# A radix-2 last step in a spectral filter: f1 of each parity in one quadrant of the array

## The chip, the cores and the metric

The kernel runs on one core of a Trainium2 chip. The core has a matrix engine (TensorE, PE in the profile), three elementwise engines (VectorE, DVE; ScalarE, ACT; GpSimd, POOL) and DMA queues, of which this kernel uses almost only the one of SyncE (SP). TensorE multiplies a stationary tile with a moving one and writes to PSUM; a matmul here has 128 rows and 128 columns of stationary data, or a half of either. The metric is device time in microseconds of one execution, lower is better.

## What is computed

The input `x` has 2048 rows (`S`) of 512 numbers (`D`). It is normalized by rows, and the result is a sum of three parts: `x` itself, a filter in the frequency domain, and a two-layer perceptron.

```python
xn  = layernorm(x)                       # rows of 512
X   = rfft2(xn) * (w_r + 1j * w_i)       # over S and D
A   = irfft2(X, (2048, 512))
h   = xn @ w1 + b1                       # 512 -> 1792
B   = (h * tanh(softplus(h))) @ w2       # 1792 -> 512
out = x + A + B
```

The transforms are written as matrix products. A row is s = 16 s1 + s2, with 128 values of s1 and 16 of s2. The last step of the inverse transform takes, for each s2, 128 numbers in the frequency f1 (64 frequencies, real and imaginary) to the 128 values of s1, for all 512 columns at once.

## The kernel before

Every operand of a matmul is a float32 number written as two float16 parts, high and low, and every product is three matmuls into one PSUM tile: high by high, high by low, low by high (`mm3`, lines L84 to L90). In the profile a product shows as one matmul each of L86, L89 and L90.

The perceptron goes in "half tiles". Four groups of 512 rows (`g`) run over 14 chunks of the hidden layer (`f`). `mlp_up` makes one chunk: twelve matmuls (L725, output `ph`), Mish on ScalarE (L733, `hb`), and the split into two float16 parts (`a`: L334 on ScalarE, L335 on VectorE). `mlp_down` takes it back: twelve matmuls (L86, L89, L90, output `pa`) into four PSUM tiles, one for each `s` of the group. `mlp_end` (L773) adds the four finished tiles to what stands in `m` (L779), and for the last group g = 3, it stores them (L781).

The filter runs beside it in steps that hand their data on through DRAM: a transform over s1 (`psS`, to `d_y`), over s2 and columns (`psP`, `psD`), the product with the weights (`spectrum`, VectorE and ScalarE), back over columns (`psA`, to `d_a`), over s2 (`psT`, `ip_unit`, to `d_t` at L707), and the last step over s1 (`psY`, `s1_inverse`, L814). `psP` already uses the array by halves of its columns (128 rows by 64 columns), and `psD` by halves of its rows (64 by 128).

`s1_inverse(g, s)` does one s2. It loads `yi` from `d_t` (L817, 256 KB in one DMA), multiplies it with the matrix `cIT` for that s2 in three matmuls of 128 x 128 by 512 columns, and VectorE adds the scaled result to a tile that already holds rows of `x`: `m` of the groups 0 to 2 (L833, loaded by `rows_back`, L771), or `y` of the group 3 (L840, loaded at L838). For the groups 0 to 2 the sum goes out at once (L834); that of group 3 waits for `mlp_end`. The tiles `psY` and those of the step before take turns in two PSUM buffers (`ps_f`), and `yi` in four SBUF buffers (`qp`, tag `q1`).

At the end of the program a loop mixes the sixteen calls of `s1_inverse` with the half tiles of the perceptron that are left: group 3 first, then 0, 1, 2, with the last calls behind the end of the perceptron. That is the order of the source. A scheduler then places the instructions on each engine and each DMA queue, and each engine and each queue works through its own list in order; an instruction at which a semaphore is waited for holds up those behind it on the same list. DMAs also take turns at eight completion semaphores (`DMAHW0` to `DMAHW7` in the lists below), and a DMA waits until the one that had its semaphore before it is done.

Of the kernel before, what the change touches and what calls it, by code (L numbers as in the profile page):

```python
# [19 lines left out]
P = 128  # L20
# [10 lines left out]
T_LAG = 4  # L31
# [8 lines left out]
def spectral_mlp_kernel(ctx, tc, x, wt, w0, w1, b1, w2, cT, cIT, cM, out):  # L40
# [16 lines left out]
    outv = out.rearrange("(p s) d -> p s d", s=NS2)  # L57
# [4 lines left out]
    d_t = dp.tile([64, P, 256], F16, tag="d_t", name="d_t")  # L62
# [134 lines left out]

    def turn(pt, xh, h):
        for dc in range(4):
            nc.tensor.transpose(pt[:, h, dc, :], xh[:, h, dc * P : (dc + 1) * P], ident)  # L200
# [10 lines left out]
    def first_group(ts):  # L211

        pe, act, dve = mybir.EngineType.PE, mybir.EngineType.Activation, mybir.EngineType.DVE
        with in_order(pe, act, dve):
# [7 lines left out]
            xTv = xnT[0].rearrange("p h c (s t) -> p h c s t", s=4)  # L222
# [26 lines left out]
            def copy(s):  # L249
                nc.vector.tensor_copy(xTv[:, 0, :, s, :], pt[s][:, 0])  # L250
                return nc.scalar.copy(xTv[:, 1, :, s, :], pt[s][:, 1])
# [31 lines left out]
    def transpose(g, s, xh):  # L283
        if s == 0:
            xnT[g] = cp.tile([P, 2, 4, 512], F16, tag=f"xnT{g}", name=f"xnT_{g}")
        xTv = xnT[g].rearrange("p h c (s t) -> p h c s t", s=4)
# [3 lines left out]
        nc.vector.tensor_copy(xTv[:, 0, :, s, :], pt[:, 0])  # L290
        nc.scalar.copy(xTv[:, 1, :, s, :], pt[:, 1])  # L291
# [397 lines left out]
    def ip_unit(c, g):  # L689
# [4 lines left out]
        for k in range(2):  # L694
# [12 lines left out]
        nc.sync.dma_start(  # L707
            d_t.rearrange("a (c f) e -> (a c) (f e)", c=2)[:, fg * 1024 : (fg + 1) * 1024],
            tt.rearrange("p l h e -> p (l h e)"),
        )  # L710
# [57 lines left out]
    def rows_back(g):  # L768

        macc[g] = cp.tile([P, 4, D], F32, tag=f"xnT{g}", name=f"m_{g}")  # L770
        nc.sync.dma_start(macc[g], xv[:, 4 * g : 4 * g + 4, :])  # L771

    def mlp_end(g):  # L773
# [3 lines left out]
        for s in range(4):  # L777
            xr = yacc[g][s] if g == 3 else m[:, s, :]
            nc.vector.scalar_tensor_tensor(m[:, s, :], pacc[g][s], sc["out"], xr, op0=ALU.mult, op1=ALU.add)  # L779
            if g == 3:  # L780
                nc.sync.dma_start(outv[:, 4 * g + s, :], m[:, s, :])  # L781
# [27 lines left out]
    def load_it():  # L809
        t = cp.tile([P, NS2, 2, P], F16, tag="cT", name="cITt")  # L810
# [3 lines left out]
    def s1_inverse(g, s):  # L814
        s2 = 4 * g + s
        yi = qp.tile([P, 4, 2, P], F16, tag="q1", name=f"yi_{s2}")
        nc.sync.dma_start(  # L817
            yi.rearrange("p a h e -> p a (h e)"),
            d_t[4 * s2 : 4 * s2 + 4].rearrange("a p e -> p a e"),
        )  # L820
        psf = ps_f.tile([P, D], F32, tag="f", name=f"psY_{s2}")
        yv = yi.rearrange("p a h (b e) -> p h b a e", b=2)
        mm3(
            psf.rearrange("p (b a e) -> p b a e", b=2, a=4),
            lambda h: sc["cIT"][:, s2, h, :],
            lambda h: yv[:, h],
            True,
            True,
            True,
        )  # L830
        if g < 3:
            m = macc[g][:, s, :]
# [349 lines left out]
```

## Time and profile before

| what | value |
|---|---|
| three timed runs | 399.61, 400.26, 400.28 us; median 400.26 |
| the profiled execution | 399.53 us, of which its span is 397.7 us |
| TensorE busy | 381.7 us, 96% of the span, 2485 matmuls |
| VectorE, ScalarE, GpSimd busy | 250.8, 200.9, 69.7 us |
| first matmul of the last step | starts at 355.63 us |
| last matmul of the perceptron | starts at 392.10 us |
| last matmul of the last step | starts at 393.40 us |
| DMA | 61.61 MB, 49.6% of the time of 16 DMA engines on the SP queue |

The span is the time from the first to the last instruction in the profile; the time of the execution is 1.83 us longer. Matmuls are pipelined: one of 512 columns is shown 379 ns long, but they start one after another every 0.216 us when TensorE waits for nothing. The busy time of a group of them is the sum of the lengths shown where others lie between, so the starts are the better measure.

### The profile page before, as it was taken

To read this page: it belongs to the slowest core of one execution; us is meant where nothing else is said; L and a number is where in the kernel's file an instruction comes from. 1 tells how busy PE (TensorE), PEld (TensorE's weight loads), DVE (VectorE), ACT (ScalarE), POOL (GpSimd) and SP (SyncE) were. 2 spreads that over 40 slices of the span, in tenths; PEclk is the share of its full clock that TensorE was granted. 3 is DMA by queue.
4 is the path that set the end of the run, shared out by engine and by line. 5 is a ranking of instruction groups with operands and counts; after the bars stand their busy time and mean duration, and the time that the engine had idled before them with its cause. 6 is when DMAs were issued, how large, how long until landed. Compare 5 with 4: busy or idle time off the path is not lost.

```text
span 397.7 us, 6578 instructions
## 1 busy us (share of the span) xinstructions
PE 381.7 (96%) x2485; PEld 191.4 (48%) x2485; DVE 250.8 (63%) x520; ACT 200.9 (51%) x325; POOL 69.7 (18%) x103
## 2 busy tenths in 40 slices
PE   8899999699998999999999999999999899999996
PEld 3444444345454454465445565455654445544442
DVE  5889777658697339843879446944439872424334
ACT  3869863576655155734646355365454474523110
POOL 0100029557565000000111101021001110220000
PEclk9999999999999999999999999999999999999999
DMA  8996015254186970353825625227471022753556
GB/s 281 363 396 258 2 53 158 81 166 151 55 297 188 271 228 3 79 134 98 255 73 144 175 54 164 77 87 200 166 190 50 27 81 70 215 171 114 173 196 253
DMA packets 49519, 61.61 MB, mean 155 GB/s; under 512 B 3776, under 2 KB 36032, under 8 KB 48848
## 3 DMA queue, kind: packets, MB, share of 16 engines
q1 hardware_dynamic: 49488, 61.20, 49.6%
q8 instruction: 19, 0.31, 0.3%
q14 instruction: 12, 0.10, 0.1%
HBM read 44.38 MB, written 16.78 MB: 154 GB/s over the span
## 4 chain that ended last, share of the span: by engine, by line
PE 54%; DVE 7%; ACT 2%; issue 2%; DMA 1%; POOL 1%; POOLq 0%; DVEq 0%; SPq 0%; ACTq 0%
PE ph L725 20%; PE pa L86 8%; PE pa L89 8%; PE pa L90 7%; PE psD L544 3%; PE psP L520 3%; DVE m L779 2%; PE psY L86 1%; PE psY L90 1%; PE psY L89 1%; PE psA L86 1%; POOL tt L129 1%; DVE a L335 1%; DMA yi<-d_t 1%; PE psA L90 1%
## 5 line engine op out<-in xcount | busy, mean ns | idle before, releaser
L725 PE MATMUL ph<-xnT,w1t 128*128 128x512 f16 x672 | 154.3, 379 | 1.9 <-ACT xnT L291 0.9
L725 PEld LDWEIGHTS <-w1t 128*128 128x128 f16 x672 | 64.7, 98 | 79.1 <-issue 2.4
L86 PE MATMUL pa<-w2r,a 128*128 128x512 f16 x224 | 84.4, 380 | 1.6 <-DVE m L779 1.4
L89 PE MATMUL pa<-w2r,a 128*128 128x512 f16 x224 | 85.0, 379 | 0.5 <-DVE w2r L335 0.5
L90 PE MATMUL pa<-w2r,a 128*128 128x512 f16 x224 | 85.0, 379 | 0.0
L335 DVE SCALAR_TENSOR_TENSOR a<-hb,sc_a,a 128x512 f16<-128x512 f32 x56 | 42.5, 761 | 56.7 <-ACT a L334 56.4
L733 ACT ACTIVATE hb<-ph,b1t,sc_exp 128x512 f32<-128x512 f32 x56 | 43.2, 771 | 59.5 <-PE ph L725 59.4
L129 POOL TENSOR_TENSOR tt<-bt_t,tt 128x512 f16<-128x512 f32 x16 | 19.6, 1230 | 195.8 <-ACT tt L128 152.9
L334 ACT ACTIVATE a<-hb,sc_a 128x512 f16<-128x512 f32 x56 | 40.1, 720 | 1.5
L90 PEld LDWEIGHTS <-a 128*128 128x128 f16 x224 | 21.9, 98 | 26.8 <-issue 1.1
L89 PEld LDWEIGHTS <-a 128*128 128x128 f16 x224 | 21.9, 98 | 25.7 <-issue 1.9
L86 PEld LDWEIGHTS <-a 128*128 128x128 f16 x224 | 21.9, 98 | 25.8 <-issue 1.2
L334 ACT ACTIVATE u<-r,sc_u 128x512 f16<-128x512 f32 x16 | 11.5, 721 | 25.3 <-DVE r L624 12.6
L129 POOL TENSOR_TENSOR y<-bt_s,y 128x512 f16<-128x512 f32 x16 | 20.1, 1261 | 18.2 <-ACT y L128 18.2
L833 DVE SCALAR_TENSOR_TENSOR m<-psY,sc_k,m 128x512 f32<-128x512 f32 x12 | 8.7, 747 | 14.9 <-PE psY L90 14.9
L128 ACT CAST tt<-bt_t 128x512 f16<-128x512 f32 x16 | 9.9, 617 | 14.9 <-DVE bt_t L126 13.4
L679 DVE SCALAR_TENSOR_TENSOR at<-psA,at 128x512 f16<-128x512 f32 x16 | 10.8, 689 | 10.4 <-ACT at L678 10.4
L128 ACT CAST y<-bt_s 128x512 f16<-128x512 f32 x16 | 9.9, 617 | 14.5 <-DVE bt_s L126 7.8
L556 ACT ACTIVATE ix<-psD 64x512 f32<-64x512 f32 x16 | 9.5, 593 | 12.8 <-PE psD L544 12.6
L678 ACT ACTIVATE at<-psA 128x512 f16<-128x512 f32 x16 | 9.2, 591 | 12.5 <-issue 7.1
L194 POOL TENSOR_TENSOR xh<-xs,xh 128x512 f16<-128x512 f32 x12 | 14.4, 1217 | 3.9 <-ACT xh L193 3.9
L544 PE MATMUL psD<-z,cMt 64*128 64x256 f16 x192 | 13.5, 270 | 1.5 <-DVE bt_t L126 1.5
(146 smaller groups left out, 510.1 us busy)
## 6 DMA issues: line engine op xcount, KB each, us to landing
wt<-in_wt_dram SPq DMA_DIRECT2D x32, 256.0 KB
x<-in_x_dram SPq DMA_DIRECT2D x8, 512.0 KB
d_y<-y SPq DMA_DIRECT2D x16, 256.0 KB
wm<-in_wt_dram SPq DMA_DIRECT2D x8, 512.0 KB
yt<-d_y SPq DMA_DIRECT2D x16, 256.0 KB
d_a<-at SPq DMA_DIRECT2D x32, 128.0 KB
ai<-d_a SPq DMA_DIRECT2D x16, 256.0 KB
d_t<-tt SPq DMA_DIRECT2D x16, 256.0 KB
```

The costliest lines, as they stand in the source:

```text
L86: first = nc.tensor.matmul(ps, stat(0), mov(0), start=start, stop=False)
L89: nc.tensor.matmul(ps, stat(0), mov(1), start=False, stop=False)
L90: return nc.tensor.matmul(ps, stat(1), mov(0), start=False, stop=stop)
L128: nc.scalar.copy(out[:, :, 0, :], tv)
L129: nc.gpsimd.tensor_sub(out[:, :, 1, :], tv, out[:, :, 0, :])
L194: nc.gpsimd.tensor_sub(xh[:, 1, :], xs, xh[:, 0, :])
L334: hi = nc.scalar.activation(dst_h, src, AF.Copy, scale=scale)
L335: lo = nc.vector.scalar_tensor_tensor(dst_l, src, scale, dst_h, op0=ALU.mult, op1=ALU.subtract)
L520: first = nc.tensor.matmul(ps[64 * be : 64 * be + 64, pr, k, :], yt[:, 2 * pr + be, hs, k, :], c_p2[:, k, v, hm, :], start=t == 0, stop=t ...
L544: first = nc.tensor.matmul(ps[be][:, k], c_d[rows, k0 + k, e, hs, :], z[rows, hm, 2 * (k0 + k) + e].rearrange("p g q -> p (g q)"), start=e ...
L725: last_mm = nc.tensor.matmul(ph, w1t[:, hs, dc, f * P : (f + 1) * P], xnT[g][:, hm, dc, :], start=n == 0, stop=n == 11)
L733: nc.scalar.activation(hb, ph, AF.Mish, bias=b1t[:, f : f + 1], scale=s_exp[k])
```

## The change

Moving s1 by 64 turns the phase of frequency f1 by f1 times a half turn. So the even f1 give the same contribution to rows s1 and s1 + 64, and the odd f1 the opposite one. The changed step works out, for 64 values of s1 only, the sum over the even f1 and the sum over the odd f1, and then adds and subtracts the two.

`s1_inverse(g, q)` now does two s2 at once (`i` = 0, 1; s2 = 4g + 2i + q), in eight calls ("units" from here on). The parity `be` of f1 chooses the half of the rows of the array (64 partitions of `yi` and `cIT`), `i` the half of the columns (64 partitions of the PSUM tile). A unit is 12 matmuls of 64 x 64 by 512 columns in place of 6 of 128 x 128, into two PSUM tiles, `ps[0]` for the even and `ps[1]` for the odd f1. ScalarE copies the odd tile with its scale to SBUF (`odd`), VectorE adds the even one to both row tiles (two operations) and then `odd` to the first, and GpSimd subtracts `odd` from the second.

The layout follows. `d_t` is split by parity, so `ip_unit` writes it in two DMAs of 128 KB, and each `yi` is read in two. The rows of a group stand in another order on the partitions, so the copies into `xnT` write runs of 64 numbers in place of 128, `rows_back` loads in two DMAs, and the stores are by 64 partitions: two DMAs for a unit in the place of two for two s2, and in `mlp_end` one on SP's and one on ScalarE's queue for each `s`. The loads of `y` stand ahead of the last loop. `cIT` has half its size. `T_LAG` goes from 4 to 2, which with 8 units in place of 16 calls means the same share of the loop.

```diff
-T_LAG = 4
+T_LAG = 2
@@ ip_unit
-        nc.sync.dma_start(
-            d_t.rearrange("a (c f) e -> (a c) (f e)", c=2)[:, fg * 1024 : (fg + 1) * 1024],
-            tt.rearrange("p l h e -> p (l h e)"),
-        )
+        for be in range(2):
+            nc.sync.dma_start(
+                d_t[be].rearrange("a (c f) e -> (a c) (f e)", c=2)[:, fg * 512 : (fg + 1) * 512],
+                tt[:, 2 * be : 2 * be + 2].rearrange("p l h e -> p (l h e)"),
+            )
@@ transpose
-        nc.vector.tensor_copy(xTv[:, 0, :, s, :], pt[:, 0])
-        nc.scalar.copy(xTv[:, 1, :, s, :], pt[:, 1])
+        pv = pt.rearrange("p h c (w t) -> p h c w t", w=2)
+        nc.vector.tensor_copy(xTv[s][:, 0], pv[:, 0])
+        nc.scalar.copy(xTv[s][:, 1], pv[:, 1])
@@ rows_back
-        nc.sync.dma_start(macc[g], xv[:, 4 * g : 4 * g + 4, :])
+        for i in range(2):
+            nc.sync.dma_start(
+                macc[g][64 * i : 64 * i + 64].rearrange("t (w q) d -> t w q d", w=2),
+                xp[:, :, 4 * g + 2 * i : 4 * g + 2 * i + 2],
+            )
@@ mlp_end
             if g == 3:
-                nc.sync.dma_start(outv[:, 4 * g + s, :], m[:, s, :])
+                for i, eng in enumerate((nc.sync, nc.scalar)):
+                    eng.dma_start(outp[:, s // 2, 4 * g + 2 * i + s % 2], m[64 * i : 64 * i + 64, s, :])
@@ s1_inverse
-    def s1_inverse(g, s):
-        s2 = 4 * g + s
-        yi = qp.tile([P, 4, 2, P], F16, tag="q1", name=f"yi_{s2}")
-        nc.sync.dma_start(
-            yi.rearrange("p a h e -> p a (h e)"),
-            d_t[4 * s2 : 4 * s2 + 4].rearrange("a p e -> p a e"),
-        )
-        psf = ps_f.tile([P, D], F32, tag="f", name=f"psY_{s2}")
-        yv = yi.rearrange("p a h (b e) -> p h b a e", b=2)
-        mm3(psf..., lambda h: sc["cIT"][:, s2, h, :], lambda h: yv[:, h], True, True, True)
+    def s1_inverse(g, q):
+        yis = []
+        for i in range(2):
+            s2 = 4 * g + 2 * i + q
+            yi = qp.tile([P, 4, 2, P], F16, tag="q1", name=f"yi_{s2}")
+            for be in range(2):
+                nc.sync.dma_start(
+                    yi[64 * be : 64 * be + 64].rearrange("p a h e -> p a (h e)"),
+                    d_t[be, 4 * s2 : 4 * s2 + 4].rearrange("a p e -> p a e"),
+                )
+            yis.append(yi.rearrange("p a h (b e) -> p h b a e", b=2))
+        ps = [ps_f.tile([P, D], F32, tag="f", name=f"psY_{g}_{q}_{be}") for be in range(2)]
+        for t, (hs, hm) in enumerate(((0, 0), (0, 1), (1, 0))):
+            for i in range(2):
+                for be in (1, 0):
+                    rows = slice(64 * be, 64 * be + 64)
+                    mm = nc.tensor.matmul(
+                        ps[be][64 * i : 64 * i + 64].rearrange("p (b a e) -> p b a e", b=2, a=4),
+                        sc["cIT"][rows, 4 * g + 2 * i + q, hs, :],
+                        yis[i][rows, hm],
+                        start=t == 0,
+                        stop=t == 2,
+                    )
+                    tc.keep_in_program_order(mm)
+        odd = tp.tile([P, D], F32, tag="bt", name=f"odd_{g}_{q}", bufs=2)
+        nc.scalar.activation(odd, ps[1], AF.Copy, scale=sc["k"])
...
+        for w in range(2):
+            nc.vector.scalar_tensor_tensor(ms[w], ps[0], sc["k"], ms[w], op0=ALU.mult, op1=ALU.add)
+        nc.vector.tensor_add(ms[0], ms[0], odd)
+        nc.gpsimd.tensor_sub(ms[1], ms[1], odd)
+        if g < 3:
+            mv = macc[g].rearrange("p (w q) d -> p w q d", w=2)
+            for i in range(2):
+                nc.sync.dma_start(outp[:, :, 4 * g + 2 * i + q], mv[64 * i : 64 * i + 64, :, q])
@@ the last loop
-    todo = [(3, s) for s in range(4)] + [(g, s) for g in range(3) for s in range(4)]
+    load_y(0)
+    load_y(1)
+    todo = [(3, q) for q in range(2)] + [(g, q) for g in range(3) for q in range(2)]
```

What the diff does not tell is where the scheduler puts the instructions. The place is the end of the program, on two lists.

First the DMA queue of SP. Before, its last entries are these (`yi_9` to `yi_11` are the inputs of the last three calls, `m_1` and `m_2` are rows of groups 1 and 2, `m_3` those of the perceptron's last group, stored by `mlp_end`; in brackets the semaphores that an entry waits for, by the engine that raises them):

```order
L817 DMA yi_10_4474<-d_t_87 128x4x256 [waits DMAHW3_49,PE_49]
L834 DMA out_0_dram<-m_1_2293 128x512 [waits DMAHW4_49,DVE_49]
L817 DMA yi_11_4482<-d_t_87 128x4x256 [waits DMAHW5_49,PE_49]
L834 DMA out_0_dram<-m_1_2293 128x512 [waits DMAHW6_49,DVE_49]
L834 DMA out_0_dram<-m_2_3385 128x512 [waits DMAHW7_49,DVE_49]
L834 DMA out_0_dram<-m_2_3385 128x512 [waits DMAHW0_49,DVE_49]
L781 DMA out_0_dram<-m_3_4465 128x512 [waits DMAHW1_49,DVE_49]
```

Now the last unit reads `yi_9` and `yi_11` in four halves, and the list ends so:

```order
L841 DMA yi_9_4583<-d_t_87 64x4x256 [waits DMAHW1_49]
L841 DMA yi_11_4586<-d_t_87 64x4x256 [waits DMAHW2_49,PE_49]
L873 DMA out_0_dram<-m_2_3395 64x2x512 [waits DMAHW3_49,DVE_49,Pool_49]
L873 DMA out_0_dram<-m_2_3395 64x2x512 [waits DMAHW5_49]
L796 DMA out_0_dram<-m_3_4570 64x512 [waits DMAHW0_49,DVE_49]
L796 DMA out_0_dram<-m_3_4570 64x512 [waits DMAHW2_49,DVE_49]
L796 DMA out_0_dram<-m_3_4570 64x512 [waits DMAHW3_49,DVE_49]
L796 DMA out_0_dram<-m_3_4570 64x512 [waits DMAHW4_49,DVE_49]
L841 DMA yi_11_4586<-d_t_87 64x4x256 [waits DMAHW5_49]
L873 DMA out_0_dram<-m_2_3395 64x2x512 [waits DMAHW6_49,DVE_49,Pool_49]
L873 DMA out_0_dram<-m_2_3395 64x2x512 [waits DMAHW7_49]
```

The last load of `yi` stood ahead of the four stores of `mlp_end`; now three halves stand ahead of them, and the second half of `yi_11` (`be` = 1, partitions 64 to 127) behind them.

Then TensorE, around the last matmul of the perceptron (`pa_3_3` is its fourth PSUM tile). Before (`psY_10` and `psY_11` take `yi_10` and `yi_11`):

```order
L90 MATMUL pa_3_3_3762<-w2r_93,a_3_13_4374 128x512
L86 MATMUL psY_10_4476<-yi_10_4474,cITt_1348 128x512
L89 MATMUL psY_10_4476<-yi_10_4474,cITt_1348 128x512
L90 MATMUL psY_10_4476<-yi_10_4474,cITt_1348 128x512
L86 MATMUL psY_11_4484<-yi_11_4482,cITt_1348 128x512
```

Now (`psY_2_1_1` is the odd tile of the last unit, `psY_2_1_0` the even one; the rows of weight loads between the matmuls are left out):

```order
L92 MATMUL pa_3_3_3775<-w2r_93,a_3_13_4463 128x512
L851 MATMUL psY_2_1_1_4590<-yi_9_4583,cITt_1349 64x512
L851 MATMUL psY_2_1_0_4589<-yi_9_4583,cITt_1349 64x512
L851 MATMUL psY_2_1_1_4590<-yi_11_4586,cITt_1349 64x512
L851 MATMUL psY_2_1_0_4589<-yi_11_4586,cITt_1349 64x512
```

In both, one pair of s2 stands behind the perceptron; before, it is two products of three, now one unit, whose third matmul is the first that reads the second half of `yi_11`. Of the other units, seven stand ahead of that place, where fourteen calls stood; two of the seven are split in two by a matmul or five of the perceptron.

47 lines of the change are left out of this document (21 added, 26 removed).

## The prediction

> **What bounds the kernel now.** I read the busy time by stretches first, then what TensorE waited for, then the chain of waits. Around the last step, by stretches (columns: length, busy time and count of PE, of its weight loads, of DVE, ACT, POOL; granted clock, DMA share, GB/s):
>
> ```profile
> 340.00:355.00 15.00, 14.66 (x79) 7.26 (x77) 4.62 (x11) 6.69 (x12) 4.58 (x4) 1.00 0.55 179
> 355.00:375.00 20.00, 19.37 (x90) 8.81 (x91) 7.33 (x10) 4.50 (x6) 0.00 (x0) 1.00 0.55 167
> 375.00:394.00 19.00, 18.78 (x87) 8.33 (x85) 9.14 (x14) 1.50 (x2) 0.00 (x0) 1.00 0.59 204
> 394.00:398.00 4.00, 0.00 (x0) 0.00 (x0) 0.63 (x1) 0.00 (x0) 0.00 (x0) 1.00 0.59 226
> ```
>
> TensorE has no room here: of 39 us it is idle for 0.85, of which 0.63 falls to the start of the step and the rest lies behind its last matmul. VectorE is busy under half of the stretch, ScalarE 6.0 us of 39, GpSimd not at all. So a matmul taken out of this stretch is time gained, and the new work on the other three is hidden as long as a matmul of the perceptron runs beside it. Only behind the last matmul is nothing hidden. The page's chain and TensorE's waits agree (the first number of a chain's row is its start, the second its length):
>
> ```profile
> 350.78 1.99 DMA d_t<-tt
> 352.86 2.64 DMA yi<-d_t
> 355.63 0.38 PE psY L86
> PE psY L86 <- DMA yi<-d_t: 0.6, 1, 0.6
> ```
>
> The step opens with two transfers in a row, a write of `d_t` and the first read of it, and TensorE waits for the second. From 355.63 on it is bound by TensorE. The end, as the timeline has it:
>
> ```profile
> 390.60 2.72 DVE L779 SCALAR_TENSOR_TENSOR m<-pa,s_out,y 128x512 f32<-128x512 f32 x4
> 391.37 2.31 SPq L781 DMA_DIRECT2D out_dram<-m  x4
> 392.10 0.38 PE L90 MATMUL pa<-w2r,a 128*128 128x512 f16 x1
> 392.32 0.38 PE L86 MATMUL psY<-yi,cITt 128*128 128x512 f16 x1
> 392.53 0.38 PE L89 MATMUL psY<-yi,cITt 128*128 128x512 f16 x1
> 392.75 0.38 PE L90 MATMUL psY<-yi,cITt 128*128 128x512 f16 x1
> 393.23 1.40 DVE L833 SCALAR_TENSOR_TENSOR m<-psY,sc_k,m 128x512 f32<-128x512 f32 x2
> 393.40 0.38 PE L90 MATMUL psY<-yi,cITt 128*128 128x512 f16 x1
> 394.00 0.99 SPq L834 DMA_DIRECT2D out_dram<-m  x2
> ```
>
> I call M the moment at which TensorE is done issuing the perceptron: 392.32. From M to the end of the span (397.7) are 5.38 us: six matmuls, the last addition (ends at 394.63 = M + 2.3), and the last store, issued at about 394.66, 3.04 us before the end.
>
> **The matmuls.** Ahead of M stand 14 products of 3 matmuls; matmuls start every 0.216 us (392.32, 392.53, 392.75), so they cost 14 x 3 x 0.216 = 9.07 us. In their place come 7 units of 12 small ones. No row shows four quadrants at work. The nearest show two halves:
>
> ```profile
> 158.12 1.42 PE psD L544 x24
> 159.54 2.70 PE ph L725 x12
> 164.83 2.59 PE ph L725 x12
> 170.01 1.46 PE psP L520 x48
> 171.47 2.70 PE ph L725 x12
> ```
>
> `psD` (halves of the rows) does 24 matmuls of 256 columns in 1.42 us; one after another they would take 24 x 0.108 = 2.59, in pairs 1.29. `psP` (halves of the columns, 128 columns) does 48 in 1.46, where pairs take 1.30. So halves run two at a time in both directions, and each burst costs some 0.13 us over the ideal, and the twelve `ph` behind it 0.11 more than elsewhere (2.70 against 2.59): 0.24 per burst. I take four at a time, since the two directions each work alone: 3 rounds x 0.216 + 0.24 = 0.89 per unit. Two units are split, so 9 bursts: 7 x 0.648 + 9 x 0.24 = 6.7 us. M moves from 392.3 to 389.9, **-2.4 us**. Bounds: bursts that cost nothing, -4.5; only two at a time, 9.07 + 2.16 = 11.2, +2.2.
>
> **The opening.** `d_t` is now written in two issues and read in two. One issue takes SP 0.33 to 0.36 us (min, median and max in ns):
>
> ```profile
> L817 SPq DMA_DIRECT2D yi<-d_t x16: 359/360/509, 352.9 to 386.0; - x16
> L781 SPq DMA_DIRECT2D out_dram<-m x4: 332/332/333, 391.4 to 393.3; - x4
> ```
>
> The second half of the last write lands that much later, 353.1; the reads that the first two small matmuls need go out at 352.86 and 353.2 and, at 2.64 each, the later one is there at 355.85. TensorE now reaches it two `ph` matmuls later (six instead of four, +0.43). The wait stays what it was: **0**, bounds -0.1 and +0.6 (a transfer more in front of the read).
>
> **Work that is hidden.** Per unit ScalarE copies `odd`, VectorE does two additions from PSUM and one from SBUF, GpSimd one subtraction. The nearest rows:
>
> ```profile
> L678 ACT ACTIVATE at<-psA 128x512 f16<-128x512 f32 x16 | 9.2, 591 | 12.5 <-issue 7.1 <-PE psA L90 5.2
> L833 DVE SCALAR_TENSOR_TENSOR m<-psY,sc_k,m 128x512 f32<-128x512 f32 x12 | 8.7, 747 | 14.9 <-PE psY L90 14.9
> L564 DVE TENSOR_TENSOR r<-r,t_c 128x512 f32<-128x512 f32 x8 | 5.5, 682 | 0.1
> L129 POOL TENSOR_TENSOR tt<-bt_t,tt 128x512 f16<-128x512 f32 x16 | 19.6, 1230 | 195.8 <-ACT tt L128 152.9
> L290 DVE COPY xnT<-pt 128x512 f16<-128x512 f16 x12 | 5.0, 415 | 0.0
> ```
>
> VectorE gets 8 x 0.68 = 5.5 us more, to 22 of 39; ScalarE 4.7; GpSimd 9.8. The PSUM tiles of a unit come free about 1.6 us after its last matmul (0.1 + 1.40, and up to 0.75 for a split L335 in between), and the next unit follows after at least one half tile of 2.59: **0**, and without that cover at most 0.9 per unit. The copies into `xnT` (L290) keep their element count: 0. Earlier in the program SP has 21 more issues (16 of `d_t`, 3 of `m`, 2 of `y`), 7 us in all; an entry behind a pair is late by 0.33 us, and TensorE's one wait there for what SP brings is short:
>
> ```profile
> PE psT L86 <- DMA ai<-d_a: 0.3, 1, 0.3
> ```
>
> I take 0, bounds 0 and +0.7.
>
> The Trainium skill has a rule that speaks against the change: "TensorEngine Tiling (Array Packing)", Performance Considerations, PSUM Bottleneck, says that tiling speeds up TensorE but not the emptying of PSUM, which can then become the bound. The rows above agree for the last unit alone; by the rule as it stands the whole stretch would be bound by VectorE, which at 22 of 39 us it is not.
>
> **The end.** Here the order decides. The second half of `yi_11` now stands on SP's list behind the four stores of `mlp_end`, and each of these waits for its VectorE addition. That a wait there holds back what stands behind is in the row of L781: four issues of 0.33 us take 2.31, the pace of the additions. The transfer rates over the span, and TensorE's longest wait, are these:
>
> ```profile
> GB/s 281 363 396 258 2 53 158 81 166 151 55 297 188 271 228 3 79 134 98 255 73 144 175 54 164 77 87 200 166 190 50 27 81 70 215 171 114 173 196 253
> PE pt L200 <- ACT xnT L291: 2.8, 1, 2.8
> ```
>
> From M on:
>
> - The fourth addition ends at 393.32, M + 1.0; the fourth store is issued then, or when the semaphore that it takes over is free. That one belongs to ScalarE's first store, issued at about M - 0.95; with the 1.99 to 2.64 that the transfers above took it is done at M + 1.0 to 1.7.
> - So `yi_11`'s second half is issued at M + 1.4 to 2.0; I take 1.7. It takes 2.64 like the first `yi`, plus up to 1.3 if the stores ahead of it (0.5 MB, at the page's highest rate) have to drain first. I take 0.4: it lands at M + 4.7. Bounds M + 3.9 and M + 5.9. TensorE has done two small matmuls by then and stands still.
> - Three more rounds, 0.65 + 0.16 until the last is through: M + 5.5. VectorE's two additions, 0.1 + 1.40: M + 7.0. GpSimd's subtraction, 0.1 + 1.23: M + 8.4. Two stores; the second is issued 0.35 later and, as before, 3.04 us before the end: **M + 11.8**, where M + 5.4 stood.
>
> **The sum.** Span: 389.9 + 11.8 = 401.7, +4.0 on 397.7. The profiled execution took 399.53, so the same one would take 403.5. It lies 0.73 below the median of the three runs (400.26), which spread from its level to that; I add half of it: **403.9 us**, slower by about 0.9%.
>
> Nothing in the rows tells what the array does after standing still for four microseconds; its longest wait before is 2.8 us, with the granted clock at 1.00 throughout. "TensorE: Matmul & The Clock Gate" of the Trainium skill, Part 1, says that after an idle window of about 3.4 us the clock drops to half. By it the three rounds would take 0.65 us more, an estimate, which would make 404.5; no run here shows it.
>
> **Rivals.**
>
> - *Two quadrants at a time instead of four.* For it: rows show pairs only. Against it: pairs work in both directions, and separately. M moves to 394.5, and the last unit takes 0.43 more (five pairs in the place of three rounds): 406.7 on the span, **about 409**.
> - *The late half doesn't hold the end.* If it lands before TensorE wants it (issued ahead of the stores, or its wait over early), the unit ends at M + 1.05, VectorE's additions at M + 2.55, GpSimd at M + 3.9, and the span at M + 7.3 = 397.2: **399.4**, faster by 0.2%, and down to 397 with bursts that cost nothing. It decides from a landing earlier than about M + 1.0. For it only that the transfer is small; against it the list, since the issue alone is not before M + 1.4.
> - *The hidden work isn't hidden.* A unit waits for the PSUM tiles of the one before, 0.9 us each at worst, in the four places where only one half tile lies between: up to +3.6 us, **about 405 to 407.5**. Against it: VectorE idles over half of the stretch.
>
> **How the numbers follow.** The forecast has 0.73; two at a time 0.08; the half that doesn't hold 0.13; hidden work that shows 0.06. The forecast's own range: -2.1 (bursts for nothing) and -0.8 (early landing) below, +1.2 (late landing), +0.6 (opening) and +0.7 (SP's issues) above, which seldom fall together: 401.2 to 406.5. The third rival reaches a little above; the first and the second stay outside: **400.9 to 407.2**. A measurement of this kernel tells 0.2% (0.8 us) from no change. Faster by more than that needs the second rival with cheap bursts: 0.07; within 0.2% the rest of it and the lowest corner: 0.08; slower 0.85.
>
> **What would show it.** In the profile after, TensorE waits once at the end for `yi` from `d_t`, 3 to 5 us, behind the last `pa`; SP issues that load behind the four stores of L796; the units ahead take about 0.9 us each (1.5 or more would mean pairs); `psY` opens at about 356; GpSimd's subtraction stands on the chain at the end. A wait of TensorE below 1 us there would make the forecast wrong, and so would units that take no less than the 1.29 us of two calls before.

## The result, and the profile after

The changed kernel takes **409.02 us** (median of six runs, 408.64 to 410.28) against 400.14 us for the kernel before (six runs, 399.61 to 400.33): a ratio of 1.023, 95% interval 1.0215 to 1.0246. It is slower by 2.3%; forecast was 0.9%. The direction and the mechanism are those of the forecast, the size is not.

The profiled execution has a span of 406.9 us. By stretches around the last step (the columns as in the prediction):

```profile
355.00:375.00 20.00, 19.16 (x125) 7.55 (x127) 11.01 (x15) 6.91 (x10) 5.23 (x4) 1.00 0.58 165
375.00:390.70 15.70, 15.70 (x96) 6.34 (x88) 8.54 (x13) 3.56 (x5) 5.82 (x4) 1.00 0.66 182
390.70:398.00 7.30, 0.98 (x11) 0.43 (x12) 1.00 (x2) 0.00 (x0) 0.00 (x0) 0.67 0.77 221
398.00:407.00 9.00, 0.97 (x10) 0.09 (x2) 2.01 (x3) 0.69 (x1) 1.57 (x1) 0.50 0.23 58
```

Up to 390.7 TensorE has no room, as before, and the new work of VectorE, ScalarE and GpSimd is hidden beside it. Then follow 16 us in which TensorE works for two. From the list of TensorE's waits (us in total, times, longest):

```profile
PE psY L851 <- DMA yi<-d_t: 7.2, 2, 6.3
```

The opening of the step and its end, from TensorE's timeline:

```profile
356.46 0.50 PE L851 MATMUL psY<-yi,cITt 64*64 64x512 f16 x2 [0.84 <-DMA yi<-d_t]
361.75 0.84 PE L851 MATMUL psY<-yi,cITt 64*64 64x512 f16 x12
390.45 0.38 PE L92 MATMUL pa<-w2r,a 128*128 128x512 f16 x1
390.76 0.40 PE L851 MATMUL psY<-yi,cITt 64*64 64x512 f16 x2
397.49 1.49 PE L851 MATMUL psY<-yi,cITt 64*64 64x512 f16 x10 [6.32 <-DMA yi<-d_t]
```

Twelve small matmuls take 0.84 us, so four quadrants do work at a time. M, when TensorE is done issuing the perceptron, is 390.45 + 0.22 = 390.67 (392.32 before). The last unit starts, stands still for 6.32 us for the second half of `yi_11`, and its ten other matmuls take 1.49 us at half clock. What led up to both, by the chain of waits, the first two rows at the opening:

```profile
352.83 0.60 SPq L841
353.60 2.73 DMA yi<-d_t
...
388.93 0.76 DVE m L793
389.71 4.29 DMA out_dram<-m
394.06 0.47 SPq L796
394.58 2.87 DMA yi<-d_t
399.01 1.42 DVE m L867 x2
```

And the lists at the end, by the timelines of SP, ScalarE, GpSimd:

```profile
388.99 1.28 SPq L873 DMA_DIRECT2D out_dram<-m  x2
390.36 4.16 SPq L796 DMA_DIRECT2D out_dram<-m  x4
389.71 3.93 ACTq L796 DMA_DIRECT2D out_dram<-m  x4
400.56 1.57 POOL L869 TENSOR_TENSOR m<-m,odd 128x512 f32<-128x512 f32 x1 [11.60 <-DVE m L867]
402.16 1.27 SPq L873 DMA_DIRECT2D out_dram<-m  x2
```

The end runs through the predicted steps: ScalarE's first store (done at 394.00), whose semaphore SP's fourth store takes over, then that store, then the load, the matmuls, the additions, the subtraction, and the two last stores, the first of them issued 4.74 us before the end.

### The profile page after: what moved, and what is told of

Read it like the earlier page. It is cut to its first block, busy times and chain, and to the rows that moved or that the text cites. A ratio compares the mean times of both kernels' runs of the same rounds, so it can differ in the third digit from the quotient of the medians.

```text
span 406.9 us, 6784 instructions
## 1 busy us (share of the span) xinstructions
PE 380.9 (94%) x2533; PEld 189.0 (46%) x2533; DVE 256.9 (63%) x528; ACT 205.9 (51%) x333; POOL 82.4 (20%) x111
## 4 chain that ended last, share of the span: by engine, by line
PE 52%; DVE 18%; ACT 10%; DMA 7%; issue 6%; POOL 5%; SPq 1%; POOLq 0%; ACTq 0%; DVEq 0%
PE ph L735 19%; PE pa L88 7%; PE pa L92 7%; PE pa L91 7%; PE psD L553 3%; PE psP L529 3%; ACT a L343 2%; ACT hb L743 2%; PE psY L851 2%; DVE xs L192 2%; DVE st L178 2%; DMA w1s<-in_w_dram 2%; DVE a L344 2%; DMA yi<-d_t 1%; POOL y L131 1%
## 5 line engine op out<-in xcount | busy, mean ns | idle before, releaser
L343 ACT ACTIVATE u<-r,sc_u 128x512 f16<-128x512 f32 x16 | 11.5, 720 | 22.2 <-DVE r L633 13.5
L860 ACT ACTIVATE odd<-psY,sc_k 128x512 f32<-128x512 f32 x8 | 5.5, 682 | 27.3 <-PE psY L851 25.1
L542 DVE SCALAR_TENSOR_TENSOR z<-psP,z 128x512 f16<-128x512 f32 x16 | 10.6, 686 | 8.9 <-ACT z L541 8.9
```

The source lines that it names most:

```text
L343: hi = nc.scalar.activation(dst_h, src, AF.Copy, scale=scale)
```

## The experiments

Theory A: the time is lost at the end, through the place of the last load and the halved transfers that put it there; the radix-2 arithmetic itself saves what it should. Theory B: the radix-2 step's own elementwise work, or halved transfers all along the last 50 us, lose it. Each result is given with its ratio to runs of the kernel before on the same chip; times apart by less than their intervals are not told apart.

### The kernel before with halved transfers only

The edit, shortened: every store of the last step and of the last rows, every write of `d_t` and every read of `yi` is split in two.

```diff
@@ ip_unit, s1_inverse, mlp_end of the kernel before
+        for be in range(2):          # d_t in two writes, yi in two reads
+            nc.sync.dma_start(yi[64 * be : 64 * be + 64]..., d_t[4 * s2 : 4 * s2 + 4, 64 * be : 64 * be + 64]...)
+                for i, eng in enumerate((nc.sync, nc.scalar)):   # each store in two
+                    eng.dma_start(outv[64 * i : 64 * i + 64, 4 * g + s, :], m[64 * i : 64 * i + 64, s, :])
```

> The kernel before with its own matmuls, in which only DMAs of the last step are halved: d_t written in two, yi read in two, each store of the last step and of the last rows in two by 64 partitions, those of the last rows on SP and ScalarE as in the change. No radix-2 step. On SP's list both halves of yi_11 now stand behind the four stores of the last rows. Theory A (the halved DMAs and where they put the last load cost the time, not the radix-2 step): the fourth of these stores waits for ScalarE's first (about 391.4 + 4.3 = 395.7), then two stores and the two halves at 0.6 each, landing at about 400.5, three matmuls at half clock, one addition, two stores: span about 407, time 407 to 410. Theory B (the radix-2 step's own elementwise work at the end costs it): 400 to 402.

Measured: 408.79 us, ratio 1.0234 (1.0213 to 1.0256), the change's own figure. From the timelines of TensorE, SP and VectorE:

```profile
392.92 0.38 PE L90 MATMUL psY<-yi,cITt 128*128 128x512 f16 x1
400.40 0.58 PE L86 MATMUL psY<-yi,cITt 128*128 128x512 f16 x1 [7.10 <-DMA yi<-d_t]
392.06 3.07 SPq L783 DMA_DIRECT2D out_dram<-m  x4
396.69 1.30 SPq L820 DMA_DIRECT2D yi<-d_t  x2
402.65 1.15 SPq L838 DMA_DIRECT2D out_dram<-m  x2
```

The same wait, behind the four stores of the last rows (and two of another tile), with no radix-2 step in the program. M, when TensorE is done issuing the perceptron, is at 392.47 here, 0.15 later than in the kernel before, so nearly all of the loss lies behind it and not along the last 50 us. This settles the main question for theory A: the halved transfers and the list order that comes with them are enough for a loss of this size. It does not show that the radix-2 step costs nothing by itself: in the change its saved matmuls and its longer chain at the end both stand in the same 2.3%.

### Moving or widening the late load

Three kernels take the load off its place. The first emits each unit's loads one unit earlier; the second lays `d_t` out as [64, 128, 256], so that one DMA reads a whole `yi`; the third loads the second half of `yi` on ScalarE's queue.

```diff
@@ loads ahead: the last loop
+        if k + 1 < n:
+            load_unit(*todo[k + 1])
@@ yi in one DMA: s1_inverse
-            for be in range(2):
-                nc.sync.dma_start(yi[64 * be : 64 * be + 64]..., d_t[be, 4 * s2 : 4 * s2 + 4]...)
+            nc.sync.dma_start(yi..., d_t[4 * s2 : 4 * s2 + 4].rearrange("a p e -> p a e"))
@@ two queues: s1_inverse
-            for be in range(2):
-                nc.sync.dma_start(
+            for be, eng in enumerate((nc.sync, nc.scalar)):
+                eng.dma_start(
```

> The changed kernel, with each unit's four loads of yi put in the source one unit earlier; on SP's list the second half of yi_11 now stands ahead of the four stores of the perceptron's last rows. Theory A (the order on SP's list makes the stall): TensorE's wait of 6.3 us for yi goes below 0.5 us and the clock stays at 1.00 to the end. The last copy of odd then stands behind ScalarE's four stores, which end at 393.6, so GpSimd ends at about 396.1, the last two stores go out at 396.2 and 396.8 and the span is 400 to 401: 401 to 403.5 us, 6 to 7 less than the change, still not below 400. Theory B (halved DMAs and the new elementwise work cost it all along the last 50 us, the wait is only where it shows): TensorE waits somewhere else instead, and the time stays at 406 or more.

> The changed kernel with d_t in another layout in DRAM, so that both parities of a yi are read in one DMA of 128 partitions (16 loads in place of 32); matmuls, stores and everything else as in the change. On SP's list the last load of yi comes to stand ahead of the four stores of the last rows. Theory A (the time goes with the place of that load): no wait of TensorE for yi above 1 us at the end, clock 1.00 there; the last odd copy still stands behind ScalarE's four stores, as in the run with the loads ahead (403.5 in its better runs). With 16 issues fewer the start of the step is 0.3 to 0.6 earlier: 402 to 403.5 us. Theory B (halved stores alone are enough for the loss): above 406.

> The changed kernel with one edit: the second half of each yi is loaded by ScalarE's queue, the first half still by SP's. SP has 16 issues of 0.6 us less in the last 50 us, and the last load of yi stands ahead of the last rows' stores on both lists. d_t, the stores and TensorE's order are as in the change. Theory A (the end is lost to the late load, and behind it to the odd copy that waits behind ScalarE's stores; the start of the step to SP's issue time): the halves go out side by side, TensorE opens the step at about 356.0 (356.46 in the change), does the perceptron by 390.3, no wait at the end, clock 1.00; from there 10.2 us to the end as in the two runs before that had no wait: span 400.5, 402 to 403 us. Theory B (halved loads cost the time wherever they are issued): 405 or more.

Measured: loads ahead 404.22 us (1.012, 1.0082 to 1.0159); one DMA 406.47 (1.0141, 1.0112 to 1.0171); two queues 402.83 (1.0097, 1.006 to 1.0133). None waits for `yi` at the end any more. With M taken as above, what lies from M to the end of the span falls from 16.2 us to 10.3, 10.2 and 10.1, as expected. The third falls in its range. The first two miss theirs by their medians, though two of the four runs of the first (403.44 and 403.47 us) lie in it; three of the four of the second are above 406, the number of its theory B. Their profiled executions (406.83 us, the highest of its four, and 406.68) lose the time at the other end of the step: it opens late, and M is 4.0 and 3.9 us later than in the change. Of the kernel with loads ahead, the chain of waits at the opening, and then the stretches:

```profile
347.46 4.03 DMA d_t<-tt
351.59 0.63 ACT tt L130
353.47 1.73 DMA d_t<-tt
355.32 0.60 SPq L842
356.08 2.74 DMA yi<-d_t
358.96 0.60 PE psY L857
```

```profile
360.00:362.00 2.00, 2.00 (x9) 0.59 (x11) 0.00 (x0) 0.00 (x0) 0.00 (x0) 0.50 0.69 199
362.00:364.00 2.00, 2.00 (x16) 0.76 (x13) 1.06 (x2) 1.03 (x2) 0.00 (x0) 0.94 0.03 7
```

A write of `d_t` takes 4.03 us where a later one takes 1.73, ScalarE waits for it to fill the next `tt` (three buffers), the step opens at 358.96 in place of 356.46 after a wait of 2.24 us, and the clock stays at half until about 362. In the kernel with one DMA it is the same (a write of 3.64 us, the opening at 358.42), and there the last write takes 2.15 us in its new layout. Why one write in some executions takes about 4 us is left open.

What then still stands behind M, in the kernel with two queues:

```profile
390.44 0.38 PE L92 MATMUL pa<-w2r,a 128*128 128x512 f16 x1
390.75 0.84 PE L851 MATMUL psY<-yi,cITt 64*64 64x512 f16 x12
389.70 3.69 ACTq L796 DMA_DIRECT2D out_dram<-m  x4
393.49 0.69 ACT L860 ACTIVATE odd<-psY,sc_k 128x512 f32<-128x512 f32 x1 [7.18 <-DMA out_dram<-m]
394.26 1.77 POOL L869 TENSOR_TENSOR m<-m,odd 128x512 f32<-128x512 f32 x1 [5.51 <-ACT odd L860]
396.05 1.30 SPq L873 DMA_DIRECT2D out_dram<-m  x2
```

`odd` is ready for its copy at 391.6, but ScalarE's list has four stores ahead of it: a second held list, behind the first. M is at 390.66, 1.66 earlier than before; the end costs 10.1 us in place of 5.4.

### Keeping the clock up

```diff
@@ s1_inverse, last unit, behind its first two matmuls
+                    for _ in range(24):
+                        mm = nc.tensor.matmul(spare, sc["cIT"][0:64, 11, 0, :], yis[0][0:64, 0], start=True, stop=True)
```

> The changed kernel with 24 matmuls more (64 rows, 64 columns, 512 moving columns, into a PSUM tile that nobody reads), on TensorE's list right behind the last unit's first two matmuls, where it waits for yi_11; about 5.2 us of work in the wait of 6.3. The order elsewhere is the same. Theory A (the clock falls because TensorE stands still, and that costs 0.7 us): the granted clock stays near 1.00 there, the last ten matmuls take 0.8 us in place of 1.49, and the time falls by 0.7, to 408.0 to 408.5 us. Theory B (the ten matmuls are slow for another reason, such as the stores beside them): 1.5 us again, and 408.8 to 409.3 us.

Measured: 409.08 us, 1.0215 (1.0199 to 1.0231), which is not told apart from the change's 1.023. Its profile tells it:

```profile
399.12 0.83 PE L853 MATMUL psY<-yi,cITt 64*64 64x512 f16 x10 [1.43 <-DMA yi<-d_t]
```

The ten matmuls take 0.83 us, not 1.49. So the halved clock comes from standing still, and costs 0.66 us. The time misses theory A's 408.0 to 408.5 all the same: in the profiled execution M is 1.35 later than in the change (392.02), and the load landed some 0.3 later counted from M, which hides half of the gain. From M to the end it took 15.9 us in place of 16.2.

### Whole stores, and an order of dimensions

```diff
@@ mlp_end
-                for i, eng in enumerate((nc.sync, nc.scalar)):
-                    eng.dma_start(outp[:, s // 2, 4 * g + 2 * i + s % 2], m[64 * i : 64 * i + 64, s, :])
+                nc.sync.dma_start(outw[g, s % 2, s // 2], m[:, s, :])
@@ first kernel: outw = out.rearrange("(w t g i q) d -> g q w i t d", ...)   # DRAM side [2][64][512]
@@ second kernel: outw = out.rearrange("(w t g i q) d -> g q w t i d", ...)  # DRAM side [64][2][512]
```

> The changed kernel, whose four last rows' stores go out whole (128 partitions, one DMA each on SP) and none on ScalarE; all else stands in the same order on SP's list, the second half of yi_11 right behind these four. Theory A (the list and, on top of it, the semaphore of ScalarE's slow first store): the fourth store is issued when its addition ends (391.7) and not at 394.06, yi_11's second half at about 392.1 and not 394.58, landing at about 395.1; TensorE waits 4.1 us and not 6.3. The rest as in the change: 2.2 to 2.6 us less, 406.4 to 406.8 us. Theory B (the stores on ScalarE and their semaphore have no part in it): 408.5 to 409.5 us. If the order alone didn't matter but only the semaphore, the wait would go below 1 us, and the time to about 402.

> As the run with the last rows' four stores whole, but on the DRAM side the dimension of 64 stands first and that of 2 second (t, i in place of i, t). The same bytes go to the same set of rows; within each group of these rows the order is another, so the rows come out in the wrong order, and only the time is read. Lists and order of all engines are the same. Theory A (a transfer is spread over as many of the 16 DMA engines as its first DRAM dimension has parts, 2 there): the four stores run at the usual rate, the fourth is issued by 392.1, yi_11's second half at about 392.1 to 392.5, and the time is what that run was to show: 406.4 to 406.8 us, 2.3 us below the change, which is then the price of the semaphore of ScalarE's first store. Theory B (it is the whole 128-partition store in this layout, whatever the order): 425 or more.

Measured: 428.29 us (1.0711, 1.0695 to 1.0727) and 409.52 us (1.0253, 1.0215 to 1.029). By stretches, the first kernel, then the second:

```profile
392.00:396.00 4.00, 0.00 (x0) 0.00 (x0) 0.00 (x0) 0.00 (x0) 0.00 (x0) 0.83 0.23 55
396.00:400.00 4.00, 0.00 (x0) 0.00 (x0) 0.00 (x0) 0.00 (x0) 0.00 (x0) 0.50 0.13 51
```

```profile
392.00:396.00 4.00, 0.00 (x0) 0.00 (x0) 0.13 (x1) 0.00 (x0) 0.00 (x0) 0.80 1.00 340
```

And of the second the chain of waits:

```profile
393.25 0.57 SPq L796
393.87 3.24 DMA yi<-d_t
397.15 1.50 PE psY L851 x9
```

With 2 as the first DRAM dimension the share of the DMA engines is 0.13, two of sixteen, at 51 GB/s; with 64 first it is 1.00 at 340. Nothing else differs (the second leaves the rows in another order, so only its time is read), so the order of dimensions costs 19 us. This was not foreseen when the first kernel was written. The Trainium skill says it: "DMA: Bandwidth & Descriptors", under "Why a DMA increments its semaphore by 16 and not by 1", has a DMA run on the largest number of engines up to 16 that divides the slowest dimension of both sides. The trace agrees.

The second kernel answers what the first was meant to ask, and against theory A's number: without any store on ScalarE the late load goes out at 393.87, M + 2.8 (M is 391.10 here), 1.1 earlier than in the change, but lands in 3.24 us and not in 2.87. The time is not told apart from the change's. TensorE goes on at M + 6.05 in place of M + 6.8. So ScalarE's stores, with the semaphore that the prediction had named, are worth 0.8 us at TensorE and nothing that the time can tell; the rest of the load's delay is the issue of SP's own stores, 0.57 to 0.82 us each here, where the prediction had 0.33.

A kernel with one DMA per `yi` and all stores whole, DRAM side [2][64][512], ran into the same at every store:

> The radix-2 step as in the change, with its DMAs at 128 partitions: d_t laid out so that each yi is read in one DMA, the stores of a unit by row half w (both i in one), the last rows stored whole on SP. The last load of yi stands ahead of the last rows' stores. Theory A (the DMAs, not the arithmetic, lose the time): TensorE's units cost 0.97 us as in the change, it is done at about 391.6 without a wait, VectorE's two additions end at 393.2, GpSimd's subtraction at 394.8, the last store goes out at 395.2 and the span is 398 to 398.5: 399.8 to 400.6 us, no better than before, since the unit behind the perceptron gives its saving back in elementwise work. Theory B (the elementwise work or the quadrants themselves lose it): 404 or more.

Measured: 465.98 us (1.1646, 1.1622 to 1.167), again at 0.13 of the DMA engines; it says nothing on its question.

### Is there a version that gains?

First, only the place of the last units (each earlier, so that one or two half tiles of the perceptron stand behind the last), with `yi` in one DMA or on two queues, and in one kernel the last rows in four stores:

```diff
@@ the last loop (E = 1, 2 or 0 half tiles more)
-        while done[0] - start < (k + T_LAG) * (total - T_HOLD - start) / n and half_tile():
+        while done[0] - start < min((k + T_LAG) * (total - T_HOLD - start) / n, total - start - (n - k) - E) and half_tile():
@@ mlp_end, four stores: s in the order 0, 2, 1, 3, a store behind the second and the fourth
+                    eng.dma_start(outp[:, :, 4 * g + 2 * i + s % 2], mv[64 * i : 64 * i + 64, :, s % 2])
```

> As the run with yi in one DMA, and the last units one half tile earlier each, so that behind the last unit there still stand two half tiles of the perceptron, which hide its additions and stores; behind the perceptron only its own four additions and eight stores (four on SP, four on ScalarE) are left. Theory A: TensorE ends at 391.6 (390.67 plus the unit that stood behind it, 0.97), the last addition at 392.5. SP's last store again takes over the semaphore of ScalarE's first, which is held 4.3 us from about 390.7, so it goes out at about 395, and the span ends at about 398.5: 400 to 401 us, no better than before. Theory B (the semaphore doesn't bind here): last stores out by 393.2, span 396.5, 398 to 399 us.

> As the run with the units earlier, but the last rows go out in four DMAs of 64 partitions by two row halves (256 KB each, two on SP and two on ScalarE) in place of eight, with the perceptron's tiles finished in the order 0, 2, 1, 3; none of the four takes over a semaphore of another. Theory A: last addition at 392.5, both last stores issued at once, done 4.1 to 4.7 us later as the last two of the change were: span 396.6 to 397.2, 398.3 to 399.2 us, 0.2 to 0.4% faster than before; the radix-2 step pays once nothing stands behind the perceptron but its own rows. Theory B (the halved stores cost the gain anyway): 400 or more.

> As the run with the two queues, and the last units earlier, so that two half tiles of the perceptron stand behind the last matmul of the last unit; of the eight last stores none takes over a semaphore of another. Theory A (the radix-2 step pays when its elementwise work and its stores are hidden): TensorE ends at 391.3, the last addition at 392.4, the last stores of 64 partitions are issued at 392.5 to 393 and done 3.3 to 4.3 later: span 396 to 397.2, 398 to 399.3 us, faster than before by 0.2 to 0.6%. Theory B (loads on ScalarE's queue hold up Mish and the split of the last tiles): TensorE waits for a by 1 us or more and the time is 400.5 or more.

> As the run before, but with only one half tile behind the last unit; the unit's stores (ready about 3.8 us after its matmuls: additions 1.5, subtraction 1.6, two issues) then still hold SP's list when the last rows are ready, and SP's last store takes over the semaphore of ScalarE's first. Theory A: the last store goes out 2 to 3 us later than in the run with two half tiles behind the unit, span 399 to 400, 400.8 to 402 us. Theory B (place and semaphores make no difference here): the same as that run within 0.5 us.

Measured: 405.60 (1.0138, 1.0107 to 1.0169), 407.27 (1.0161, 1.0135 to 1.0188), 405.26 (1.0142, 1.0101 to 1.0183) and 405.70 us (1.0125, 1.0093 to 1.0158). All four expected less. The first, second and fourth open the step late as above (357.99, 358.50 and 357.72). In the third TensorE is done only at 394.94, even in its profiled execution, which is the lowest of its six (403.18 us): it waits for `yi` for 2.7 us in all, and its order breaks the last unit into pieces of one, two and nine matmuls between those of `pa`, so that in the first two pieces the four quadrants are not all at work. And where the units stand earlier, their stores hold SP's list when the last rows are ready; the kernel with one half tile behind, on SP's queue:

```profile
388.21 8.11 SPq L873 DMA_DIRECT2D out_dram<-m  x6
396.41 4.16 SPq L796 DMA_DIRECT2D out_dram<-m  x4
```

Then whole stores with 64 first (rows in the wrong order), with the load on two queues, in the order of the change and with one half tile behind the last unit; the edit is that of the section above, for the units' stores too:

> As the run with yi's halves on two queues, with all stores of the last step and of the last rows whole, 128 partitions each, all on SP, the DRAM dimension of 64 first (rows in the wrong order, as above, so only the time is read). Nothing of ScalarE's stands ahead of the last odd copy now. Theory A: TensorE is done with the perceptron at 390.7, the last unit's subtraction ends at 394.7, the last store goes out at 395.1 and is done 3.0 later as in the kernel before: span 398 to 398.5, 400 to 400.6 us; the radix-2 step with whole transfers breaks even. Theory B (stores make no difference): 402.4 to 403.

> As the run before, with one half tile of the perceptron behind the last unit. Theory A: TensorE ends at 391.6; the last rows' additions wait for the unit's and end at 393.9, the last store is done at 397.2: 398.8 to 399.4 us, 0.2 to 0.3% faster than before. Theory B (the place of the last unit makes no difference): the same as the run before.

Measured: 401.51 us (1.0039, 1.0024 to 1.0053) and 401.83 (1.0048, 1.0034 to 1.0063). Both expected less, the first by 0.9 to 1.5 us and the second by 2.4 to 3.0. Whole stores are worth 1.3 us against two queues alone, the place of the last unit nothing that the times can tell. Last, again with the loads on two queues, the step in seven units, and the last unit summed in PSUM, so that no copy, no addition from SBUF and no subtraction follow:

```diff
@@ s1_inverse, (g, q) = (2, 1)
+            for w in range(2):
+                for t, (hs, hm) in enumerate(((0, 0), (0, 1), (1, 0))):
+                    for i in range(2):
+                        wt = sc["cIT"][:, 9 + 2 * i, hs, :] if w == 0 else sc["neg"][:, i, hs, :]   # odd rows negated
+                        nc.tensor.matmul(ps[w][64 * i : 64 * i + 64]..., wt, yis[i][:, hm], start=t == 0, stop=t == 2)
```

> As the run with the two queues; in the last unit alone both parities are summed in PSUM (12 matmuls of 128 rows and 64 columns, two columns halves at once, with a negated copy of the odd rows of cIT for the lower half of the rows), so no odd copy, no addition from SBUF and no subtraction on GpSimd follow it. Its result goes out in four stores of 128 KB, two on each queue. Theory A (the chain behind the last matmul costs: odd waits for ScalarE's stores, then 0.7 + 1.6, then the stores): perceptron done at 390.7, last addition at 393.2, but each queue has six stores of 0.6 and waits for semaphores among them, as the four took until 394 in the run with two queues; last store issued at about 394.6, done 3.3 later: span 398 to 398.6, 400 to 400.6 us. Theory B (the chain costs nothing, only the stores do): 402.4 to 403.

> As the run before, with the last rows in four stores of 256 KB in place of eight of 128 KB (the perceptron's tiles finished in the order 0, 2, 1, 3), so that each queue has four stores at the end and none waits for another's semaphore among them. Theory A: last addition at 393.2, last store issued at 393.3 to 393.8, done 3.3 to 4 later: span 396.6 to 397.8, 398.6 to 399.8 us, even with the kernel before or up to 0.3% faster. Theory B (the count of stores does not matter): within 0.5 us of the run before.

Measured: 401.70 us (1.0046, 1.0026 to 1.0065) and 401.63 (1.0038, 1.0023 to 1.0052): theory A's numbers are missed by 1.1 to 1.7 and by 1.8 to 3.0 us, and fewer stores make no difference. These two are the best of the kernels with all rows in their place, and still 0.4 to 0.5% slower than before. The end of the second, by the timelines of TensorE, VectorE and SP:

```profile
391.18 0.38 PE L92 MATMUL pa<-w2r,a 128*128 128x512 f16 x1
392.37 1.41 DVE L865 SCALAR_TENSOR_TENSOR m<-psY,sc_k,m 128x512 f32<-128x512 f32 x2
393.15 2.97 SPq L867 DMA_DIRECT2D out_dram<-m  x2
```

The last addition ends at 393.78, M + 2.4, as in the kernel before (M + 2.3). From it to the end of the span (399.8) are 6.0 us, where 3.1 stood: the two stores behind it, on each queue, keep SP until 396.12, at 1.42 and 1.46 us for each issue. With whole stores and the long chain it is the other way round: the subtraction ends at M + 4.1, and 4.2 us follow. So each of the two, the chain behind the last matmul and the stores, is alone enough to take back what the matmuls save. Both cures at once were not tried, since whole stores put the rows in the wrong order.

## Why the prediction was right or wrong

Direction, mechanism and chain were right: four quadrants at a time, hidden elementwise work, one wait at the end, the load behind the four stores, GpSimd on the chain. The first rival (pairs) is refuted by 0.84 us for twelve matmuls, the second (the half that doesn't hold the end) by the wait of 6.32, the third by 15.70 busy of 15.70 us up to M. The wait itself, 6.32 us, is longer than the 3 to 5 that the forecast named as its sign. The time fell out of the range above, because terms of the sum were too small, nearly all with one sign:

| step | predicted | measured | off by |
|---|---|---|---|
| M against before | -2.4 | -1.65 | +0.75 |
| second half of `yi_11` issued | 1.7 | 3.9 | +2.2 |
| landed, TensorE goes on | 4.7 | 6.8 | -0.1 |
| matmuls through | 5.5 | 8.3 | +0.7 |
| VectorE's two additions done | 7.0 | 9.8 | -0.05 |
| GpSimd done | 8.4 | 11.5 | +0.3 |
| end of the span | 11.8 | 16.2 | +1.4 |

Below the first row all is counted from M; the last column is what each step adds to the error, 5.2 us together: a span of 406.9 in place of 401.7.

- **The matmuls** are nearly right. From the opening to M it took 36.69 us before and takes 34.21 now; two `ph` (0.43) moved ahead of the opening, so the seven units save 2.05 of the 2.4 forecast, at 1.00 each. The opening, put at 0, cost the other 0.4: its wait is 0.2 longer, since one issue of a half `yi` takes 0.60 us and not 0.36, and TensorE gets there 0.2 later.
- **The issue times** are the step that failed. I priced each new DMA by rows of transfers over 128 partitions (L817 and L781). The new ones have 64 on the SBUF side, and the profile before had such rows, which I did not use (min, median and max in ns):

```profile
L684 SPq DMA_DIRECT2D d_a<-at x32: 574/616/1425, 180.4 to 340.9; - x32
```

In the change a half `yi` takes 0.6 us to issue, a store of the unit before 0.62, and those of the last rows this (the same three numbers):

```profile
L796 SPq DMA_DIRECT2D out_dram<-m x4: 466/638/1593, 390.4 to 394.1; - x4
```

Two stores of the unit before and three of the last rows, one of them the 1.59, stand nearly back to back on SP's list from 388.99 on, and the third is through only at M + 2.75. That is 1.6 of the 2.2. At the very end two issues of 0.6 follow one another, and from the second to the end are 4.1 us where I took 3.04: the +1.4. "DMA: Bandwidth & Descriptors" of the Trainium skill, Rules for kernel authors, advises against two transfers to disjoint halves of the partitions and for one over 128; the kernel before with halves agrees, at +2.3%, though by its issues and its list and not by the shared DMA engines that the page gives as the reason. It was the rule that spoke against this change, and the prediction weighed another one.
- **ScalarE's first store** is the other 0.6 of the 2.2: it took 4.29 us, where I put 1.99 to 2.64 from rows of a write of `d_t` and a read of `yi`. Its semaphore came at M + 3.3, when SP had stood still for it for 0.6 us (from the list of SP's waits):

```profile
SPq L796 <- DMA out_dram<-m: 0.6, 1, 0.6
```

The 1.1 that the load gained in the kernel with 64 first is more than this wait, since there SP issued all four stores in 3.06 us, in which it issued three in the change.
- **The clock** fell to 0.50, by the rule that the prediction named and left out of its sum. With TensorE kept busy the ten matmuls take 0.66 us less.
- **GpSimd's subtraction** takes 1.57, not the 1.23 of a row with another output type.

The range already added up all the upper bounds that the prediction had (+1.2, +0.6 and +0.7, to about 406.4), and 409.02 lies above that. TensorE went on 0.9 us beyond the bound for the late landing (M + 5.9). The clock, the subtraction and the last stores, 2.4 us together, had no bound at all: the subtraction and the last stores were each taken from a single row, and the clock was left out of the sum. That the opening, the late load and the last stores all erred upward has a common cause, the halved transfers.

## What to carry to other kernels

When a step is cut in halves by partitions, price its DMAs by rows of the same shape, and so of the same partition count: twice as many issues, each nearly twice as long, are over three times the time on a queue's list. Ask of every list at the end of a program what stands behind the last stores, for there no other work hides it; a gain of 2 us in matmuls is gone with one late load. And give each term of a sum a bound of its own: what has none is missing from the range.

## What was not expected of the hardware

- A DMA of 256 KB whose DRAM pattern begins with a dimension of 2 ran on 0.13 of the DMA engines at 51 GB/s, against 1.00 at 340 GB/s with 64 first (19 us in this program).
- Issuing a DMA over 64 partitions mostly takes SP 0.57 to 0.64 us (but 1.59 once at the end of the change, and 1.42 and 1.46 at the end of the last kernel above; why is left open), over 128 partitions with evenly spaced rows mostly 0.33 to 0.36; one over 128 partitions with a DRAM side of [64][2][512] takes 0.56 to 0.82 too, so it is not the partition count alone.
- After a wait of only 2.24 us the clock stood at 0.50 for some 3 us (kernel with loads ahead; after 2.83 us in the one with one DMA for `yi` it fell as well), while TensorE's wait of 2.8 us for `xnT` leaves the profile before at 1.00. "TensorE: Matmul & The Clock Gate" of the Trainium skill, Part 1, has a window that runs freely, of 3.4 us; a wait shorter than it, with a half clock after it, does not fit the plain form of that rule.
